# 64-bit weights made float32 by two VectorE instructions instead of three, and a gate made one ScalarE instruction

## The chip, the core and the metric

The kernel runs on one core of a Trainium2 chip. The core has five engines with a queue of instructions each, which runs in order: TensorE (PE, with its weight loads as PEld), VectorE (DVE), ScalarE (ACT), GpSimd (POOL) and SyncE (SP), which here only issues DMA transfers. They wait for one another by semaphores. The metric is the device time of one execution in microseconds (us); lower is better.

## What is computed

Attention with a block-causal mask over 4 batches, 8 heads, 576 positions and a head dimension of 64, then two feed-forward layers over the 2304 tokens. q, k, v are float32; the weights arrive as float64.

```python
scores = scale * np.matmul(q, k.transpose(0, 1, 3, 2))
scores = np.where(block_i >= block_j, scores, -1000000000.0)      # blocks of 64 positions
attn = softmax(scores)                                            # with 1e-9 added to the sum
x = heads_joined(attn @ v)                                        # 2304 x 512
h = x @ w_in;  g = np.maximum(h, 0.0) + alpha * np.minimum(h, 0.0);  x = g @ w_out      # layer 1: 512 x 2048, 2048 x 512
h = x @ w_in2; g = h * (1.0 / (1.0 + np.exp(-1.702 * h)));           out = g @ w_out2   # layer 2, same sizes
```

## The kernel before

**Number formats.** A float32 value is multiplied as a high and a low part (fp32r), three matmuls for each product. A weight tile of 128 x 512 arrives as 64-bit words (`load_w`, tile `rw`, 512 KB, two buffers). `narrow` (L163 to L179) makes it float32 in tile `sq`. A 64-bit float has 1 sign bit, 11 exponent bits and 52 fraction bits; its upper word (`wf[:, :, 1]`, every other 32-bit word of `rw`) holds all but the low 32 fraction bits. ScalarE scales the upper word, taken as a float32, by a power of two, which rebases the exponent (L171); VectorE shifts it left by 3 and masks (L174), puts the sign back (L176), and adds the top 3 bits of the lower word `wi[:, :, 0]` (L177). The integer scratch `wa` shares a tag of two buffers with other weight scratch. `split_w` or `comb` then make the high and low parts. There are 64 weight tiles, 32 of each layer.

**Stages.** (1) Attention, pass by pass (20 passes); beside it, as filler for TensorE, half of layer 1 in blocks of 288 tokens (`gemm1`, `gate`, `gate_split`, `g2_half`; eight of its sixteen slices of 128 hidden units), whose result goes to a DRAM scratch `xa`. A pass goes: scores on TensorE (L448), row extremes on VectorE (L462), exponentials on ScalarE (L472), and from pass 8 on high and low halves (L568, L573) in tile `hl`, which a transposing DMA (L577, issued by SP) turns into `pt`, and the product with v on TensorE (L599). (2) The other half of layer 1 in five units of up to 512 tokens, by a Strassen-like scheme with combined weights and inputs (tiles `ws`, `xc`; matmuls L843 into `ga` and `ep`; sums L891 to L894); `g2` (L918) accumulates into four `acc` banks of PSUM, and `block_out` adds what stage 1 left in `xa` (loaded to tile `o`, L927; added by VectorE, L928; stored to `x2s`, L929). The next unit's `g2` may write an `acc` bank only after that add; `o` has two buffers. (3) Layer 2 in five units of eight pairs of slices, in the same scheme.

**The gate.** `gate` (L232 to L242) makes g of h. Layer 1: ScalarE writes max(-h, 0) to `g`, VectorE combines it with h. Layer 2: ScalarE writes sigmoid(1.702 h) to `g` (L240), VectorE multiplies by h into the PSUM bank (L241). `gate_split` then has ScalarE write the high part of it (L140) and VectorE or GpSimd the low part (L143).

**What sets the order.** The code is recorded step by step with `at(kind, n, ...)`; each kind has a due place, shifted by a table of numbers `SHIFT`. `arrange` then runs a list scheduler with a cost for each instruction, and binds every engine's order to the result. So an engine's order is fixed when the program is built: an instruction whose input is late holds up all that stand behind it on its engine. Early in stage 1, 104 `warm` matmuls that compute nothing stand between the others.

Of the kernel before, what the change touches and what calls it, by code (L numbers as in the profile page):

```python
# [15 lines left out]
ACTF = mybir.ActivationFunctionType  # L16
ALU = mybir.AluOpType
# [40 lines left out]
    "split x 2": 8, "turn": 1.5, "turn out": 4.6, "pv t": 2, "sum t": 2.2, "sum out": 4.6, "out t": 4.5, "scale t": 5, "load w": 9, "load w 2": 9, "load x": 9, "load k": 9.5, "load q": 9.5, "load v": 9.5, "load alpha": 9.6,  # L58
}
SHIFT = {  # L60
    "comb 2": 232.8, "comb 3": -27.9, "first": 27.3, "gate": -98.0, "gate 0": -19.6, "gate 2": 67.8,
    "gemm1": 68.3, "gemm1 0": 171.6, "gemm2": 27.6, "half": 66.8, "half 0": 164.8, "half out": -68.7,
    "half out 0": 90.2, "high": 37.1, "load alpha": -25.6, "load k": 97.5, "load k 0": -174.1, "load q": 31.3,
    "load q 0": 127.5, "load v": -31.6, "load v 0": 140.7, "load w": -98.2, "load w 2": -24.0,
    "load w 3": 13.9, "load wc": -36.6, "load x": 132.4, "narrow": 100.5, "narrow 2": 19.6, "narrow 3": 96.5,
    "norm": 32.7, "norm 0": 111.8, "out": 26.7, "out t": -34.5, "prep out": 33.8, "prep out 0": 43.8,
    "prep t": 63.8, "prep t 0": -50.0, "prep v": 92.2, "pv": -64.1, "pv out": -63.9, "pv t": 43.2,
    "rest": -30.8, "scale t": 6.7, "score": -10.7, "score 0": -166.4, "second": 27.7, "setup": -15.8,
    "setup 2": -29.8, "snap": 1.4, "soft": -70.8, "soft 0": 17.8, "split g": -167.4, "split g 0": 68.9,
    "split g 2": 45.0, "split w": -71.7, "split w 2": 46.4, "split w 3": 58.0, "split x": 35.9,  # L70
    "split x 2": 84.1, "sum out": -41.5, "sum t": 28.5, "sums": -46.2, "turn": -70.2, "turn out": -30.2,
    "warm": 50.2,
}
BIG = 1.0e30

# [2 lines left out]
def kernel(  # L78
# [30 lines left out]
    scale = 1.0 / float(D) ** 0.5  # L109

    pe, dve, act, pool, sp = nc.tensor, nc.vector, nc.scalar, nc.gpsimd, nc.sync
# [51 lines left out]
    def narrow(u):  # L163

        src = words[u]
        wi = src.bitcast(I32).rearrange("p (n t) -> p n t", t=2)
        wf = src.bitcast(F32).rearrange("p (n t) -> p n t", t=2)
        sq = raw.tile([128, 512], F32, tag="sq", name="sq")  # L170
        act.activation(out=sq, in_=wf[:, :, 1], func=ACTF.Copy, scale=2.0 ** -112)  # L171
        hi = sq.bitcast(I32)
        a = raw.tile([128, 512], I32, tag="wc", bufs=2, name="wa")
        dve.tensor_scalar(out=a, in0=hi, scalar1=3, scalar2=0x7FFFFFF8, op0=ALU.logical_shift_left,  # L174
                          op1=ALU.bitwise_and)
        dve.scalar_tensor_tensor(out=a, in0=hi, scalar=-0x80000000, in1=a, op0=ALU.bitwise_and, op1=ALU.bitwise_or)  # L176
        dve.scalar_tensor_tensor(out=hi, in0=wi[:, :, 0], scalar=29, in1=a, op0=ALU.logical_shift_right,  # L177
                                 op1=ALU.bitwise_or)
        words[u] = sq  # L179

    def split_w(u, lo):
# [15 lines left out]
    pend = {}  # L197
# [11 lines left out]
    turn = []  # L209
# [22 lines left out]
    def gate(key, layer, f):  # L232
        ps, n = pend[key, f]
        g = gbuf(key, "g")[:, 0:n]
        to = ps if key[0] else g
        if layer == 0:
            act.activation(out=g, in_=ps, func=ACTF.Relu, scale=-1.0)
            dve.scalar_tensor_tensor(out=to, in0=g, scalar=nalph[:, f:f + 1], in1=ps, op0=ALU.mult, op1=ALU.add)  # L238
        else:
            act.activation(out=g, in_=ps, func=ACTF.Sigmoid, scale=1.702)  # L240
            dve.tensor_tensor(out=to, in0=g, in1=ps, op=ALU.mult)  # L241
        pend[key, f] = (to, n)  # L242

    def gate_split(key, f, lo, z=None):
        g, n = pend.pop((key, f))
# [178 lines left out]
    first = []  # L424
    place_ = []
    n = 0
# [183 lines left out]
    for u, (i, g, prods, part) in enumerate(slots):  # L610
        n = place_[u]
# [183 lines left out]
    wc = {}  # L795
# [456 lines left out]
```

## Time and profile before

| | |
|---|---|
| median of 3 runs | 1005.78 us (1004.87 to 1006.44) |
| profiled execution, its own time | 1003.02 us |
| span of its trace | 1001.2 us |
| mean granted TensorE clock | 0.998 of full speed |
| busy: PE | 978.1 us (98%) |
| busy: PEld, DVE | 859.7, 651.0 us |
| busy: ACT, POOL | 533.7, 351.9 us |
| HBM traffic over the span | 177 GB/s |

The profile is one execution. Busy time is the union of an engine's instructions; the time between them is idle, and the trace names what ended it. A view by stretches gives the busy time of every engine in each window; a view of waits gives who waited for whom; the timeline gives the instructions in order, with the idle time ahead of one in square brackets.

### The profile page before, as it was taken

Reading aid. Unit: us, or ns where it says so; the run is one execution under the profiler, and the core shown is the slowest. Engines: PE = TensorE matmul, PEld = TensorE weight load, DVE = VectorE, ACT = ScalarE, POOL = GpSimd, SP = SyncE. Lnnn points to the kernel's source line nnn. Section 1 sums busy time; section 2 is a strip of 40 time slices with the busy share of each in tenths; the row PEclk is TensorE's granted clock in tenths of the full one; section 3 lists DMA queues with packets and bytes.
Section 4 is the critical chain, followed back from the end, with each engine's and each line's share of the span. In section 5 each row is a group of like instructions: output and inputs, shape, how many; then the busy total and the mean of one; then the engine's idle time right before and its main releaser. Section 6 shows DMA issues by size and latency. Waiting matters only on the chain.

```text
span 1001.2 us, 21866 instructions
## 1 busy us (share of the span) xinstructions
PE 978.1 (98%) x8260; PEld 859.7 (86%) x8260; DVE 651.0 (65%) x1301; ACT 533.7 (53%) x1284; POOL 351.9 (35%) x396
## 2 busy tenths in 40 slices
PE   8999999999999999999999999999999999999998
PEld 5777787787788999999899889889999899899997
DVE  4788877786577566778778797887535534534332
ACT  4778777775777455565445555555423423433232
POOL 4346243442625156753426535233311311211000
PEclk9999999999999999999999999999999999999999
DMA  9635999999986866654656688987745756564360
GB/s 191 161 124 142 209 211 205 206 204 213 192 201 131 169 210 218 243 190 167 206 171 230 231 274 273 315 302 248 238 160 181 256 165 198 195 207 145 98 208 32
DMA packets 234648, 198.31 MB, mean 198 GB/s; under 512 B 146224, under 2 KB 172848, under 8 KB 234544
## 3 DMA queue, kind: packets, MB, share of 16 engines
q1 hardware_dynamic: 233216, 196.60, 69.2%
q8 instruction: 65, 1.06, 0.5%
q10 hardware_dynamic: 1328, 0.33, 0.2%
q14 instruction: 39, 0.32, 0.1%
HBM read 136.32 MB, written 40.89 MB: 177 GB/s over the span
## 4 chain that ended last, share of the span: by engine, by line
PE 81%; DMA 9%; ACT 3%; DVE 2%; POOL 2%; SPq 1%; issue 1%; POOLq 0%; ACTq 0%; DVEq 0%
PE acc L918 28%; PE ga L843 15%; PE ep L843 11%; PE h L223 7%; PE pv L599 3%; PE sc L448 3%; DMA pt<-hl 3%; PE x L268 3%; PE x L269 3%; PE x L270 3%; DMA wc<-wc 3%; PE pv L524 2%; PE tp L388 1%; DMA o<-xa 1%; PE s L448 1%
## 5 line engine op out<-in xcount | busy, mean ns | idle before, releaser
L918 PE MATMUL acc<-wh,gs 128*128 128x512 f32 x576 | 184.5, 391 | 2.1 <-DVE o L928 2.1
L843 PE MATMUL ga<-xc,ws 128*128 128x256 f32 x1368 | 184.2, 283 | 0.0
L843 PEld LDWEIGHTS ga<-xc,ws 128*128 128x128 f32 x1368 | 176.5, 191 | 4.6
L843 PE MATMUL ep<-xc,ws 128*128 128x256 f32 x936 | 130.7, 283 | 0.0
L918 PEld LDWEIGHTS acc<-wh,gs 128*128 128x128 f32 x576 | 108.3, 188 | 24.6 <-DVE o L928 2.9
L869 POOL TENSOR_TENSOR v<-u,v 128x256 f32<-128x256 f32 x48 | 40.5, 843 | 239.4 <-ACT v L868 239.3
L843 PEld LDWEIGHTS ep<-xc,ws 128*128 128x128 f32 x936 | 120.4, 192 | 0.4
L918 PE MATMUL acc<-wl,gs 128*128 128x512 f32 x288 | 112.6, 391 | 0.0
L867 ACT ACTIVATE u<-ga 128x512 f32<-128x512 f32 x48 | 28.6, 596 | 146.3 <-PE ga L843 146.3
L918 PE MATMUL acc<-gs,wh 128*128 128x512 f32 (+1 forms) x320 | 92.2, 371 | 2.1 <-DVE o L928 2.1
L891 DVE TENSOR_TENSOR u<-ep,v 128x256 f32<-128x256 f32 x48 | 20.2, 421 | 112.0 <-PE ep L843 111.7
L143 POOL TENSOR_TENSOR gs<-g,gs 128x288 fp32r<-128x288 f32 x64 | 56.1, 881 | 100.8 <-ACT gs L140 95.8
L223 PE MATMUL h<-xh,wh 128*128 128x288 f32 x256 | 78.8, 308 | 1.2 <-DVE g L238 1.1
L268 PE MATMUL x<-gs,wh 128*128 128x288 f32 x256 | 76.9, 304 | 0.5 <-ACT xo L274 0.3
L223 PE MATMUL h<-xlb,wh 128*128 128x288 f32 x256 | 77.1, 301 | 0.0
L269 PE MATMUL x<-gs,wh 128*128 128x288 f32 x256 | 76.2, 299 | 0.5 <-POOL gs L143 0.5
L223 PE MATMUL h<-xh,wl 128*128 128x288 f32 x256 | 76.4, 298 | 0.0
L270 PE MATMUL x<-gs,wl 128*128 128x288 f32 x256 | 76.1, 300 | 0.0
L462 DVE TENSOR_REDUCE stat<-sc 128x1 f32<-128x384 f32 (+7 forms) x128 | 55.1, 457 | 24.0 <-PE sc L448 22.2
L472 ACT ACTIVATE e<-sc,stat 128x384 f32<-128x384 f32 (+7 forms) x128 | 64.1, 511 | 7.4 <-DVE stat L462 6.6
L822 POOL TENSOR_TENSOR xt<-xr 128x512 f32<-128x512 f32 x40 | 55.2, 1389 | 35.6 <-DVE xc L143 13.5
L918 PEld LDWEIGHTS acc<-gs,wh 128*128 128x128 f32 x320 | 56.8, 189 | 11.2 <-DVE o L928 2.7
(118 smaller groups left out, 2146.6 us busy)
## 6 DMA issues: line engine op xcount, KB each, us to landing
ws<-wc SPq DMA_DIRECT2D x284, 256.0 KB, 3.9
wc<-wc SPq DMA_DIRECT2D x84, 256.0 KB, 3.3
rw<-in_moe_w_in_dram SPq DMA_DIRECT2D x32, 512.0 KB, 4.4
rw<-in_moe_w_out_dram SPq DMA_DIRECT2D x32, 512.0 KB, 4.1
xa<-xo SPq DMA_DIRECT2D x32, 144.0 KB, 3.3
out_dram<-o SPq DMA_DIRECT2D x18, 256.0 KB, 2.4
nat_k<-in_k_dram SPq DMA_DIRECT2D x32, 128.0 KB, 3.0
vt<-in_v_dram SPq DMA_DIRECT2D x32, 128.0 KB, 3.3
```

What stands on the lines that cost most here:

```text
L143: eng.tensor_tensor(out=dst, in0=src, in1=hi.bitcast(F32), op=ALU.subtract)
L223: pe.matmul(ps, st_[:, sl], mv[:, c], start=z == 0, stop=z == 3 * KD - 1)
L268: pe.matmul(ps, oh[:, sl], gh, start=f == 0, stop=False)
L269: pe.matmul(ps, oh[:, sl], gl, start=False, stop=False)
L270: pe.matmul(ps, ol[:, sl], gh, start=False, stop=f == NA - 1)
L448: pe.matmul(to[x:x + 64], qs[64 * h:64 * h + 64, 64 * y:64 * y + 64], ks[64 * h:64 * h + 64, k0:k0 + n], start=True, stop=True)
L462: dve.tensor_reduce(out=stat[:, 0, a:a + 1], in_=v, op=ALU.min, axis=AX.X if y < 8 else AX.XY)
L472: act.activation(out=eo if y < 8 else eo.rearrange("p (a b) -> p a b", a=2), in_=v, func=ACTF.Exp, scale=-1.0, bias=stat[:, 0, a:a + 1], a ...
L822: pool.tensor_tensor(out=x, in0=y, in1=y2, op=op)
L843: pe.matmul(ps, st_, mv, start=first and z == 0, stop=last and z == 5, skip_group_check=True)
L869: pool.tensor_tensor(out=v, in0=u[:, TH:TB], in1=v, op=ALU.subtract)
L918: pe.matmul(ps, a, b_, start=first and z == 0, stop=last and z == 2)
```

## The change

`narrow`: the ScalarE step becomes a leaky ramp (Prelu): a value of zero or more is scaled by 2^-112 as before, a negative one by 2^-112 times 2^32. The factor for negative values moves the exponent up by 32, so that after the shift left by 3 the sign bit comes out set; the instruction that put the sign back is gone. The remaining two on VectorE are a shift-and-mask of the lower word, which reads the 64-bit tile itself, and a shift-and-or. The tile `rw` is now read by the first VectorE instruction and not by the last.

`gate`, layer 2: ScalarE computes h times sigmoid(1.702 h) at once (Gelu_apprx_sigmoid) into `g`; the VectorE product is gone, `gate_split` reads `g` in SBUF and not the PSUM bank.

`SHIFT` has new values throughout, so `arrange` gives other orders on all engines. The instructions are otherwise the same in number and kind on PE, ACT, POOL and SP; DVE has 1157 instead of 1301.

```diff
-    "comb 2": 232.8, "comb 3": -27.9, "first": 27.3, "gate": -98.0, "gate 0": -19.6, "gate 2": 67.8,
...
+    "comb 2": -11.2, "comb 3": -22.2, "first": 27.1, "gate": -19.0, "gate 0": 39.3, "gate 2": -90.1,
...
-        act.activation(out=sq, in_=wf[:, :, 1], func=ACTF.Copy, scale=2.0 ** -112)
+
+        act.activation(out=sq, in_=wf[:, :, 1], func=ACTF.Prelu, scale=2.0 ** -112, alpha=2.0 ** 32)
         hi = sq.bitcast(I32)
         a = raw.tile([128, 512], I32, tag="wc", bufs=2, name="wa")
-        dve.tensor_scalar(out=a, in0=hi, scalar1=3, scalar2=0x7FFFFFF8, op0=ALU.logical_shift_left,
-                          op1=ALU.bitwise_and)
-        dve.scalar_tensor_tensor(out=a, in0=hi, scalar=-0x80000000, in1=a, op0=ALU.bitwise_and, op1=ALU.bitwise_or)
-        dve.scalar_tensor_tensor(out=hi, in0=wi[:, :, 0], scalar=29, in1=a, op0=ALU.logical_shift_right,
-                                 op1=ALU.bitwise_or)
+        dve.tensor_scalar(out=a, in0=wi[:, :, 0], scalar1=29, scalar2=7, op0=ALU.logical_shift_right, op1=ALU.bitwise_and)
+        dve.scalar_tensor_tensor(out=hi, in0=hi, scalar=3, in1=a, op0=ALU.logical_shift_left, op1=ALU.bitwise_or)
...
-        to = ps if key[0] else g
         if layer == 0:
             act.activation(out=g, in_=ps, func=ACTF.Relu, scale=-1.0)
+            to = ps if key[0] else g
             dve.scalar_tensor_tensor(out=to, in0=g, scalar=nalph[:, f:f + 1], in1=ps, op0=ALU.mult, op1=ALU.add)
-        else:
-            act.activation(out=g, in_=ps, func=ACTF.Sigmoid, scale=1.702)
-            dve.tensor_tensor(out=to, in0=g, in1=ps, op=ALU.mult)
-        pend[key, f] = (to, n)
+            g = to
+        else:
+            act.activation(out=g, in_=ps, func=ACTF.Gelu_apprx_sigmoid)
+        pend[key, f] = (g, n)
```

Three places show how the orders moved. Lines of the changed kernel are three lower than before from `gate` on, and buffers have other numbers.

TensorE, where the accumulators pass from the third full unit of layer 1 to the fourth (near 585 us of the trace). `acc_8815` to `acc_8817` are the first three banks, `acc_8767` to `acc_8769` the same banks in the changed kernel; `ga`, `ep` are matmuls of the scheme. Before:

```order
L918 MATMUL acc_8815<-gs_163,wh1_6123 128x512 x2
L918 MATMUL acc_8815<-gs_163,wl1_6124 128x512
L918 MATMUL acc_8816<-gs_163,wh1_6123 128x512 x2
L918 MATMUL acc_8816<-gs_163,wl1_6124 128x512
L843 MATMUL ga_8773<-xc_8512,ws_6936 128x256 x6
L843 MATMUL ga_8773<-xc_8515,ws_6932 128x256 x4
L918 MATMUL acc_8817<-gs_163,wh1_6093 128x512 x2
```

Changed:

```order
L915 MATMUL acc_8768<-gs_163,wh1_6097 128x512 x2
L915 MATMUL acc_8768<-gs_163,wl1_6098 128x512
L840 MATMUL ga_8725<-xc_8466,ws_6898 128x256 x6
L840 MATMUL ga_8725<-xc_8469,ws_6894 128x256 x6
L840 MATMUL ep_8726<-xc_8474,ws_6892 128x256 x6
L915 MATMUL acc_8767<-gs_163,wh1_6126 128x512
L915 MATMUL acc_8768<-gs_163,wh1_6126 128x512
L915 MATMUL acc_8769<-gs_163,wh1_6068 128x512 x2
```

The third bank is first written behind 10 matmuls of 256 columns before, behind 18 of them and two of 512 columns now.

VectorE, where the accumulators pass from layer 1 to layer 2 (near 630 us). `o_9292` and `o_9236` are the third of the unit's four adds; L174, L176, L177 (now L174, L175) are `narrow`; L891 to L894 (now L888 to L891) are sums of a pair. Before:

```order
L174 TENSOR_SCALAR wa_9033<-sq_9031 128x512
L143 TENSOR_TENSOR gs_163<-ep_9213,gs_163 128x512
L176 SCALAR_TENSOR_TENSOR wa_9033<-sq_9031,wa_9033 128x512
L174 TENSOR_SCALAR wa_9160<-sq_9158 128x512
L177 SCALAR_TENSOR_TENSOR sq_9031<-rw_8985,wa_9033 128x512
L176 SCALAR_TENSOR_TENSOR wa_9160<-sq_9158,wa_9160 128x512
L891 TENSOR_TENSOR u_9424<-ep_9355,v_9425 128x256
L143 TENSOR_TENSOR wl1_9043<-sq_9031,wh1_9042 128x512
L892 TENSOR_TENSOR u_9424<-u_9424,ga_9354 128x256
L893 TENSOR_TENSOR ep_9355<-ep_9355,u_9424 128x256
L894 TENSOR_TENSOR ga_9354<-ga_9354,u_9424 128x256
L928 TENSOR_TENSOR o_9292<-acc_8817,o_9292 128x512
```

Changed:

```order
L175 SCALAR_TENSOR_TENSOR sq_9147<-sq_9147,wa_9149 128x512
L889 TENSOR_TENSOR u_9222<-u_9222,ga_9156 128x256
L890 TENSOR_TENSOR ep_9157<-ep_9157,u_9222 128x256
L891 TENSOR_TENSOR ga_9156<-ga_9156,u_9222 128x256
L142 TENSOR_TENSOR wl1_9153<-sq_9147,wh1_9152 128x512
L142 TENSOR_TENSOR gs_163<-g_9277,gs_163 128x512
L142 TENSOR_TENSOR gs_163<-g_9279,gs_163 128x512
L925 TENSOR_TENSOR o_9236<-acc_8769,o_9236 128x512
L174 TENSOR_SCALAR wa_9246<-rw_9196 128x512
L175 SCALAR_TENSOR_TENSOR sq_9244<-sq_9244,wa_9246 128x512
L925 TENSOR_TENSOR o_9240<-acc_8770,o_9240 128x512
L888 TENSOR_TENSOR u_9364<-ep_9295,v_9365 128x256
```

The third add stood behind the sums of the next pair (`ep_9355`); it now stands ahead of them (`ep_9295`), and so does the fourth.

VectorE, first pass of attention (near 10 us): `sc_281` are its scores, `rw_605` is the first weight tile, `sq_655` what ScalarE makes of it. Before:

```order
L462 TENSOR_REDUCE stat0_189<-sc_281 128x1 x2
L406 COPY k0_266<-tp_292 128x384
L462 TENSOR_REDUCE stat0_189<-sc_281 128x1 x3
L500 COPY pe_375<-et_347 128x128
L174 TENSOR_SCALAR wa_657<-sq_655 128x512
```

Changed:

```order
L459 TENSOR_REDUCE stat0_189<-sc_281 128x1 x3
L403 COPY k0_266<-tp_292 128x384
L459 TENSOR_REDUCE stat0_189<-sc_281 128x1
L174 TENSOR_SCALAR wa_657<-rw_605 128x512
L459 TENSOR_REDUCE stat0_189<-sc_281 128x1
```

The first instruction on a weight tile now waits for the transfer of `rw` itself and not for ScalarE, and stands between reductions of the scores.

## Rows read from the trace of the kernel before

**Rows 1.** Windows: stretch, length, busy time (count) per engine, clock, DMA, GB/s.

```profile
0.00:25.00 25.00, 20.91 (x157) 13.31 (x157) 11.35 (x33) 11.17 (x34) 11.43 (x36) 0.94 0.94 191
25.00:125.00 100.00, 97.92 (x1051) 76.81 (x1050) 83.40 (x179) 75.31 (x190) 40.12 (x44) 1.00 0.62 159
125.00:275.00 150.00, 141.91 (x1932) 114.70 (x1934) 107.20 (x257) 108.35 (x315) 63.30 (x69) 1.00 1.00 206
...
575.00:650.00 75.00, 70.86 (x447) 63.54 (x446) 62.76 (x111) 38.70 (x74) 28.81 (x30) 1.00 0.85 285
650.00:950.00 300.00, 300.00 (x1879) 272.23 (x1879) 153.85 (x281) 115.51 (x221) 63.96 (x71) 1.00 0.62 201
950.00:1001.00 51.00, 47.20 (x286) 42.00 (x284) 15.17 (x39) 17.17 (x45) 0.00 (x0) 1.00 0.37 119
sum 1001.00, PE 978.07 PEld 859.73 DVE 650.99 ACT 533.71 POOL 351.91; mean PE 122.26 PEld 107.47 DVE 81.37 ACT 66.71 POOL 43.99
```

**Rows 2.** Waits of PE: who waited for whom, us in total, times, longest.

```profile
PE pv L599 <- DMA pt<-hl: 5.9, 6, 1.8
PE acc L918 <- DVE o L928: 4.1, 4, 1.7
```

**Rows 3.** Timeline of PE: start, length, what, count [idle before <- what ended it].

```profile
174.81 1.39 PE L599 MATMUL pv<-pt,vp 128*64 128x256 f16 x43 [1.72 <-DMA pt<-hl]
...
587.40 0.73 PE L918 MATMUL acc<-gs,wh 128*128 128x512 f32 x2 [1.60 <-DVE o L928]
...
589.13 0.88 PE L843 MATMUL ep<-xc,ws 128*128 128x256 f32 x6
589.85 1.60 PE L843 MATMUL ga<-xc,ws 128*128 128x256 f32 x12
...
592.15 0.73 PE L918 MATMUL acc<-gs,wh 128*128 128x512 f32 x2 [0.46 <-DVE o L928]
...
636.45 0.50 PE L918 MATMUL acc<-wh,gs 128*128 128x512 f32 x1 [1.71 <-DVE o L928]
```

**Rows 4.** Groups of DVE: instruction, count | busy us, mean ns | idle before.

```profile
L177 DVE SCALAR_TENSOR_TENSOR sq<-rw,wa 128x512 int32<-128x512 int32 x64 | 53.0, 828 | 1.2
L176 DVE SCALAR_TENSOR_TENSOR wa<-sq,wa 128x512 int32<-128x512 int32 x64 | 52.1, 814 | 1.2
...
L174 DVE TENSOR_SCALAR wa<-sq 128x512 int32<-128x512 int32 x64 | 30.9, 483 | 17.3 <-ACT sq L171 12.6 <-DMA wc<-wc 3.2 <-DMA o<-xa 0.7
L241 DVE TENSOR_TENSOR ga<-g,ga 128x512 f32<-128x512 f32 (+1 forms) x40 | 25.7, 642 | 30.2 <-ACT g L240 30.1
L241 DVE TENSOR_TENSOR ep<-g,ep 128x512 f32<-128x512 f32 (+1 forms) x40 | 25.5, 637 | 0.8 <-ACT g L240 0.6
```

**Rows 5.** Windows, instructions of L174 alone: stretch, length, DVE busy (count), clock, DMA.

```profile
25.00:125.00 100.00, 8.32 (x16) 1.00 0.62 159
125.00:275.00 150.00, 1.77 (x4) 1.00 1.00 206
...
575.00:650.00 75.00, 4.58 (x10) 1.00 0.85 285
```

**Rows 6.** Timeline of SP, DMA issues in the stretch 160 to 176 us.

```profile
166.54 2.24 SPq L158 DMA_DIRECT2D rw<-in_moe_w_in_dram  x1
168.88 3.81 SPq L577 DMA_TRANSPOSE pt<-hl  x1
```

**Rows 7.** Timeline of DVE in the stretch 630 to 642 us.

```profile
633.79 0.42 DVE L891 TENSOR_TENSOR u<-ep,v 128x256 f32<-128x256 f32 x1
...
635.72 0.68 DVE L928 TENSOR_TENSOR o<-acc,o 128x512 f32<-128x512 f32 x1
```

**Rows 8.** Waits of ACT for weight transfers: us in total, times, longest.

```profile
ACT sq L171 <- DMA rw<-in_moe_w_out_dram: 8.9, 8, 3.2
...
ACT sq L171 <- DMA rw<-in_moe_w_in_dram: 7.3, 5, 2.4
```

**Rows 9.** Group of ACT on the weight words.

```profile
L171 ACT ACTIVATE sq<-rw 128x512 f32<-128x512 f32 x64 | 42.2, 669 | 16.9 <-DMA rw<-in_moe_w_out_dram 8.9 <-DMA rw<-in_moe_w_in_dram 7.3 <-DVE wl L143 0.7
```

More of the change, by code (lines that the diff above doesn't have):

```diff
@@ L60 @@
 SHIFT = {
-    "comb 2": 232.8, "comb 3": -27.9, "first": 27.3, "gate": -98.0, "gate 0": -19.6, "gate 2": 67.8,
[L62 to L72, printed above, removed]
+    "comb 2": -11.2, "comb 3": -22.2, "first": 27.1, "gate": -19.0, "gate 0": 39.3, "gate 2": -90.1,
+    "gemm1": 75.3, "gemm1 0": 264.6, "gemm2": 27.4, "half": 73.5, "half 0": 154.4, "half out": -8.9,
+    "half out 0": -68.9, "high": 65.0, "load alpha": -19.0, "load k": 11.5, "load k 0": -144.8,
+    "load q": 41.1, "load q 0": -3.3, "load v": 46.5, "load v 0": 85.1, "load w": -131.1, "load w 2": -0.6,
+    "load w 3": 48.6, "load wc": -35.6, "load x": -10.8, "narrow": 23.3, "narrow 2": 28.9, "narrow 3": -94.2,
+    "norm": 80.0, "norm 0": 112.9, "out": 8.8, "out t": -0.1, "prep out": 42.0, "prep out 0": -35.2,
+    "prep t": 76.8, "prep t 0": 120.4, "prep v": 4.3, "pv": 64.5, "pv out": -57.6, "pv t": 17.6, "rest": -6.9,
+    "scale t": -52.2, "score": -106.3, "score 0": -69.4, "second": 27.1, "setup": -36.2, "setup 2": 7.2,
+    "snap": -30.4, "soft": 3.7, "soft 0": -48.3, "split g": -11.9, "split g 0": 4.8, "split g 2": -32.6,
+    "split w": 38.7, "split w 2": 16.6, "split w 3": 25.7, "split x": -2.9, "split x 2": 41.2,
+    "sum out": -15.1, "sum t": -31.8, "sums": -37.0, "turn": -96.8, "turn out": 2.1, "warm": 60.0,
 }
```

## The prediction

> **What bounds the kernel now.** I read the windows by stage first [rows 1], because a share over the whole span mixes stages with different limits. TensorE is busy 978.1 us of a span of 1001.2, so only 23.1 us are idle. They lie in five places: 25.00 - 20.91 = 4.1 us in the first 25 us, 2.1 from 25 to 125, 8.1 from 125 to 275, 4.1 from 575 to 650, and 3.8 behind the last matmuls (the rest has 0.9 in all). From 650 to 950 TensorE is busy for 300.00 of 300.00 us. VectorE, which the change relieves, is the busiest of the others where attention runs beside the weight work (83.40 of 100 us) and around 600 us (62.76 of 75), but it is no bound by itself in any stage. So the change is worth what it takes from TensorE's waits, and no more.
>
> The view of TensorE's waits [rows 2] then says which of them VectorE feeds. 5.9 us go to the transposing DMAs that bring the attention weights to L599, 4.1 us to the add L928 that frees an accumulator bank. The first ends on a DMA, the second on VectorE. The timeline shows single ones: 1.72 us ahead of L599, and 1.60, 0.46 and 1.71 us at two changes of unit [rows 3].
>
> **The first part, narrow.** Each weight tile costs VectorE 483 + 814 + 828 ns = 2.13 us in three instructions, and 64 of them 136 us [rows 4]. Afterwards it is one instruction on one tile and one on two. The second has the form of L176, 814 ns. The first has the form of L174 (483 ns) but reads every other word, as L177 does in one of its inputs (828 ns). These are the two ends: the relief is between 2.13 - 1.64 = 0.48 us and 2.13 - 1.30 = 0.83 us for a tile. I take 0.81, near the upper end, because L177 with its stride costs only 14 ns more than L176 without one; a stride of two words hardly shows there. That is 52 us of VectorE in all, of which 16 tiles or 13 us from 25 to 125, 4 tiles or 3 us from 125 to 275, and 10 tiles or 8 us from 575 to 650 [rows 5]. All of it lies beside TensorE's work.
>
> L177 reads every other word at the pace of L176 [rows 4]. [...]
>
> On ScalarE one instruction takes the place of one. The trace has no Prelu; the nearest row is the Copy on the same words, 669 ns [rows 9]. If it cost nothing more, nothing changes; if it cost twice as much, ScalarE would have 16 x 0.67 = 10.7 us more from 25 to 125, 86 of 100 us [rows 1], still below VectorE now. I take 669 ns. Both orders hold two table loads, so no switch of tables is added.
>
> The tile `rw` is now let go by the first VectorE instruction, at least 0.81 us earlier. What stands behind its next load is the SP queue: from 166.54 us a weight load held SP for 2.24 us, and the transposing DMA behind it was issued at 168.88 [rows 6]; TensorE waited 1.72 us at 174.81 [rows 3]. This is a real lever on the 5.9 us, but only 4 of the 64 tiles fall from 125 to 275 [rows 5].
>
> **The second part, the gate of layer 2.** It takes 80 products off VectorE, 25.7 + 25.5 = 51.2 us [rows 4]. Nearly all of them lie between 600 and 1001 us, where TensorE does not wait: cost and gain zero. The cover is the 300.00 us of TensorE's work; VectorE has 153.85 of them and ScalarE 115.51 [rows 1]. The low part now reads two SBUF tiles instead of one in PSUM; even if each of the 80 took as long again as the product that is gone, VectorE would be where it was. The PSUM banks come free earlier, and nobody waits for them there.
>
> **The third part, the orders.** TensorE's instructions are the same in number and kind, so its busy time stays; I leave it at 978.1. What moves are the waits.
>
> From 575 to 650: at the change of unit near 587 us the third bank is written behind 8 more matmuls of 256 columns and two of 512. Six of the former take 589.85 - 589.13 = 0.72 us [rows 3], 0.12 each; with two of double width that is 8 x 0.12 + 2 x 0.24 = 1.4 us more cover for a wait of 1.60, and the fourth bank's 0.46 us goes with it. I keep 0.2. At the change near 636 us the third add ran at 635.72, behind the sums of the next pair, whose first started only at 633.79 [rows 7]. In the new order it stands ahead of them, so it can run up to 1.9 us sooner; but TensorE asks for that bank 31 matmuls of 256 columns, 3.7 us, sooner as well (it stood behind 42 of them, now behind 11). The loads of `o`, too, stand nearer to the stores ahead of them on SP. Between all covered, 0, and 1.71 + 3.7 - 1.9 = 3.5 us I take 1.4 for this change. So the stretch keeps 1.6 of 4.1 us: -2.5, with ends of -4.1 and -0.4.
>
> From 125 to 275: the same chain from scores over VectorE and SP to L599 is planned again, with 3 us less on VectorE and a weight load that holds SP for less time. I take -1.0 of 8.1; the ends are -4 (half of the waits go) and +4 (half as much again, since the orders differ throughout).
>
> From 25 to 125: VectorE goes from 83 to 70 us of 100. Of 2.1 us I take 0.5 off, with ends of -2.1 and +2.
>
> The first 25 us and the last 3.8 us: the same loads, the same filler matmuls, the same last matmuls and stores. I take 0, with 1 us either way for the loads' order.
>
> The sum is -2.5 - 1.0 - 0.5 = -4.0 us. The profiled execution took 1003.02 us, 1.8 more than its span of 1001.2, and so would come to 999.0. The median of the runs is 2.8 above that execution, and the prediction is for the median: 1005.8 - 4.0 = **1001.8 us**.
>
> **The rivals.**
> No change: the new orders pay what the old ones paid. For it: most of the idle time in the attention stage ends on DMAs [rows 2], not on VectorE, and there are few tiles there. Then 125 to 275 keeps 8.1, 25 to 125 keeps 2.1, and from 575 to 650 the worse end holds, 0.2 + 3.5 = 3.7: -0.4, or 1005.4 us. Against it: the order at both changes of unit moved the way that the waits ask for.
>
> Slower: VectorE stands before weights that have not landed. Its first instruction on a tile now waits for the transfer itself, and in the first pass it stands between two reductions of the scores; what is queued behind it is the softmax, and TensorE behind that. ScalarE waited for such transfers 13 times, 16.2 us in all, 1.25 us each [rows 8]. The place is 25 to 125 us. VectorE would have 100 - 70.4 = 29.6 us to spare there, or 1.85 us for each of 16 tiles, and from that point on it delays TensorE one for one. At 1.25 us it costs nothing. At 2.4 us, the longest wait for an input weight, it costs 16 x 2.4 - 29.6 = 8.8 us, and with the other -3.5 the time is 1011.1. Against it: 1.25 is well under 1.85, and an earlier freed `rw` lets loads start sooner.
>
> Larger gain: half of the waits from 125 to 275 go (-4), all from 575 to 650 (-4.1), half from 25 to 125 (-1): 996.7 us. For it: both are fed by VectorE or by SP behind it.
>
> That the strided instruction is slow (828 ns, relief 0.48 us) is a rival of the mechanism but not of the time: VectorE still has 16 x 0.48 = 8 us less to do from 25 to 125, and the forecast moves by some tenths.
>
> **How the numbers follow.** Forecast 0.48, own range 1000 to 1004; no change 0.24; slower 0.16; larger gain 0.12. The prediction is the forecast's, 1001.8. A measurement of this kernel can tell about 0.2%, 2.0 us. Faster by more: 0.48 + 0.12, less the edge of the forecast that falls inside, 0.58. Within: 0.24. Slower by more: 0.16 and the upper edge of no change, 0.18. For 8 in 10 I go from 996, which leaves out less than half of the larger gain, to 1009.5, which leaves out most of the slower case.
>
> **What would show it.** In the profile of the changed kernel: the first instruction of `narrow` near 0.5 us and the second near 0.8; VectorE near 550 us busy; TensorE still near 978; PE's wait for L925 (the add) at 1 to 2 us instead of 4.1, and for the transposing DMA near 5; 300 of 300 us from 650 to 950. The forecast is wrong if TensorE's waits for the transposing DMAs or for VectorE's reductions grow by more than 4 us, if VectorE idles behind `rw`, or if the stage from 650 on shows idle time on TensorE.

## The result, and the profile of the changed kernel

The changed kernel takes 1017.88 us (median of 4 runs, 1015.71 to 1020.61) against 1005.33 us (4 runs): a ratio of 1.0128, 95% interval 1.0096 to 1.0161. It is slower by 12.5 us, where the prediction had 4 us faster and a range that ended at 1009.5. The profiled execution took 1015.71 us with a span of 1013.9.

Windows of the changed kernel, as [rows 1]: stretch, length, busy time (count) of PE, PEld, DVE, ACT, POOL, then clock, DMA, GB/s.

```profile
0.00:25.00 25.00, 19.28 (x155) 12.51 (x156) 10.53 (x30) 10.47 (x31) 11.46 (x35) 1.00 0.94 187
25.00:125.00 100.00, 96.06 (x1034) 74.75 (x1034) 69.45 (x168) 76.06 (x195) 41.30 (x44) 0.98 0.67 171
125.00:275.00 150.00, 138.24 (x1818) 113.70 (x1816) 105.79 (x245) 105.72 (x312) 66.53 (x69) 0.98 0.92 210
275.00:350.00 75.00, 75.00 (x927) 63.06 (x928) 44.48 (x111) 48.10 (x139) 22.75 (x25) 1.00 0.64 126
350.00:575.00 225.00, 221.94 (x1664) 209.14 (x1661) 149.23 (x266) 117.97 (x266) 114.86 (x121) 1.00 0.61 200
575.00:650.00 75.00, 69.45 (x431) 61.87 (x430) 54.35 (x96) 37.31 (x71) 34.19 (x32) 1.00 0.86 295
650.00:950.00 300.00, 300.00 (x1885) 272.51 (x1884) 118.37 (x215) 117.05 (x225) 71.29 (x72) 1.00 0.62 203
950.00:1014.00 64.00, 60.26 (x364) 53.71 (x363) 13.07 (x30) 19.68 (x50) 0.74 (x1) 1.00 0.37 115
sum 1014.00, PE 980.22 PEld 861.24 DVE 565.27 ACT 532.37 POOL 363.13; mean PE 122.53 PEld 107.65 DVE 70.66 ACT 66.55 POOL 45.39
```

Length less PE's busy time, stretch by stretch, against [rows 1], gives where the 12.7 us of span come from:

| stretch | idle before | idle after | difference | predicted |
|---|---|---|---|---|
| 0 to 25 | 4.1 | 5.7 | +1.6 | 0 |
| 25 to 125 | 2.1 | 3.9 | +1.9 | -0.5 |
| 125 to 275 | 8.1 | 11.8 | +3.7 | -1.0 |
| 275 to 575 | 0.7 | 3.1 | +2.3 | 0 |
| 575 to 650 | 4.1 | 5.6 | +1.4 | -2.5 |
| 650 to the end | 4.0 | 3.6 | -0.4 | 0 |
| PE's busy time | 978.1 | 980.2 | +2.1 | 0 |

VectorE has 86 us less to do, and TensorE waits more in nearly every stage. Its waits, as [rows 2]:

```profile
PE pv L596 <- DMA pt<-hl: 9.7, 8, 3.1
PE acc L915 <- DVE o L925: 4.4, 3, 2.6
PE x L265 <- DVE g L235: 3.6, 3, 2.1
PE et L487 <- ACT e L469: 2.7, 3, 1.8
```

The longest is 3.1 us for a transposing DMA at 205 us. Timelines of the changed kernel there; first PE (start, length, what, count [idle before <- what ended it]):

```profile
200.27 1.19 PE L445 MATMUL sc<-ks,qt 64*64 64x288 f32 x8 [1.09 <-ACT e L469]
...
204.99 1.28 PE L596 MATMUL pv<-pt,vp 128*64 128x128 f16 x20 [3.08 <-DMA pt<-hl]
```

then the last VectorE work on that DMA's input, and SP's issues:

```profile
183.83 1.63 DVE L570 SCALAR_TENSOR_TENSOR hl<-e,stat,hl 128x448 f16<-128x448 f32 x2
```

```profile
181.95 4.37 SPq L574 DMA_TRANSPOSE pt<-hl  x1
...
188.86 1.05 SPq L356 DMA_DIRECT2D nat_q<-in_q_dram  x2
189.96 4.69 SPq L574 DMA_TRANSPOSE pt<-hl  x1
...
197.07 0.55 SPq L157 DMA_DIRECT2D rw<-in_moe_w_in_dram  x1
197.67 3.48 SPq L574 DMA_TRANSPOSE pt<-hl  x1
```

The input was complete at 183.83 + 1.63 = 185.46 us. SP came to the transposing DMA at 197.67, 12.2 us later: two other transposing DMAs of 4.37 and 4.69 us, and loads and stores, stood ahead. This wait of TensorE comes from the SP queue's order; a faster VectorE would not have shortened it. Matched in the same way by the order of the program, three more of the waits (121.68, 162.78 and 196.04 us) have an input that was ready 6.2 to 7.8 us before SP came to it. Not all are SP's: at 147.31 us, a wait of 0.7 us, SP came 0.6 us after the input.

The granted clock of the same place, in windows:

```profile
195.00:202.45 7.45, 4.84 (x74) 3.64 (x72) 4.67 (x12) 5.39 (x21) 2.83 (x4) 1.00 0.85 195
202.45:209.28 6.83, 4.29 (x49) 4.22 (x50) 2.57 (x6) 0.83 (x2) 1.51 (x2) 0.50 0.86 223
```

After a wait of 1.09 us and in the middle of that of 3.08 us the clock fell to 0.50 until 209.28. The matmuls of L220 with 288 columns start 0.24 us apart there (207.41 to 208.85 us) and 0.13 us apart behind it (210.14 to 211.86 us). By that, an estimate, about half of the 4.29 us busy there is added time, which is most of the +2.1 us of PE's busy time. (One stretch of 3.4 us at half clock between 21 and 29 us, in which TensorE is busy throughout, stands in both traces and cancels.) The wait is paid twice.

The instructions of `narrow` and of the low part, group by group (count | busy us, mean ns | idle before), as [rows 4] and [rows 9]:

```profile
L142 DVE TENSOR_TENSOR gs<-g,gs 128x512 fp32r<-128x512 f32 (+1 forms) x80 | 55.1, 699 | 90.4 <-ACT gs L139 90.4
...
L175 DVE SCALAR_TENSOR_TENSOR sq<-sq,wa 128x512 int32<-128x512 int32 x64 | 52.7, 825 | 6.0 <-ACT sq L171 4.9
...
L174 DVE TENSOR_SCALAR wa<-rw 128x512 int32<-128x512 int32 x64 | 36.7, 573 | 32.3 <-DMA rw<-in_moe_w_out_dram 19.0 <-DMA rw<-in_moe_w_in_dram 6.3 <-DMA wc<-wc 4.9
```

```profile
L171 ACT ACTIVATE sq<-rw 128x512 f32<-128x512 f32 x64 | 42.4, 676 | 29.6 <-DMA rw<-in_moe_w_out_dram 18.0 <-DMA rw<-in_moe_w_in_dram 10.8 <-POOL wc L742 0.5
```

### The profile page after: what moved, and what is told of

It is laid out like the page before. It is cut to its first block, busy times and chain, and to the rows that moved or that the text cites. A ratio compares the mean times of both kernels' runs of the same rounds, so it can differ in the third digit from the quotient of the medians.

```text
span 1013.9 us, 21666 instructions
## 1 busy us (share of the span) xinstructions
PE 980.2 (97%) x8260; PEld 861.2 (85%) x8260; DVE 565.3 (56%) x1157; ACT 532.4 (53%) x1284; POOL 363.1 (36%) x396
## 4 chain that ended last, share of the span: by engine, by line
PE 70%; DMA 12%; DVE 6%; ACT 5%; issue 2%; POOL 2%; SPq 2%; DVEq 0%; ACTq 0%; POOLq 0%
PE acc L915 25%; PE ga L840 13%; PE ep L840 9%; PE h L220 6%; DMA wc<-wc 5%; PE pv L596 3%; PE sc L445 3%; PE x L265 3%; PE x L266 2%; PE x L267 2%; DMA pt<-hl 2%; DMA rw<-in_moe_w_out_dram 2%; DMA rw<-in_moe_w_in_dram 2%; SPq L356 1%; ACT e L469 1%
## 5 line engine op out<-in xcount | busy, mean ns | idle before, releaser
L142 DVE TENSOR_TENSOR gs<-g,gs 128x512 fp32r<-128x512 f32 (+1 forms) x80 | 55.1, 699 | 90.4 <-ACT gs L139 90.4
L139 ACT ACTIVATE gs<-g 128x288 fp32r<-128x288 f32 (+2 forms) x144 | 74.3, 525 | 15.9 <-DVE g L235 14.6
L220 PE MATMUL h<-xh,wh 128*128 128x288 f32 x256 | 79.6, 311 | 0.2 <-DVE g L235 0.2
L888 DVE TENSOR_TENSOR u<-ep,v 128x256 f32<-128x256 f32 x48 | 20.2, 420 | 105.6 <-PE ep L840 105.6
L220 PE MATMUL h<-xlb,wh 128*128 128x288 f32 x256 | 77.8, 304 | 0.0
L220 PE MATMUL h<-xh,wl 128*128 128x288 f32 x256 | 76.9, 301 | 0.0
L596 PEld LDWEIGHTS <-vp 128*64 128x64 bf16 x1680 | 46.7, 112 | 24.1 <-issue 13.2
```

The costliest lines, as they stand in the source:

```text
L139: act.activation(out=dst, in_=src, func=ACTF.Copy, scale=scale_)
L142: eng.tensor_tensor(out=dst, in0=src, in1=hi.bitcast(F32), op=ALU.subtract)
L220: pe.matmul(ps, st_[:, sl], mv[:, c], start=z == 0, stop=z == 3 * KD - 1)
L596: pe.matmul(o, l, r, start=z < 2, stop=z >= len(ops) - 2)
```

## The experiments

The change has three parts: the two edits, and a table that gives every engine another order. Theory A: the order costs, the edits don't. Theory B: the edits cost, because VectorE now stands before weights that have not landed (25.3 us of idle time ahead of L174 above). To tell them apart, a kernel can have its orders written down in place of planned ones; `placed` returns an engine's instructions in a recorded order:

```diff
+    orders = {e: placed(e, todo) for e in names}
     for order in orders.values():
         for a, b in zip(order, order[1:]):
```

All runs have both edits unless another code is named, and each is compared with the kernel before on the same chip.

| run | code | order | us, median | ratio to before (95%) |
|---|---|---|---|---|
| f1 | both edits | before | 1007.70 | 1.0018 (0.9995 to 1.0040) |
| f2 | narrow alone | before | 1005.92 | 1.0018 (0.9996 to 1.0039) |
| f3 | gate alone | changed | 1062.60 | 1.0565 (1.0534 to 1.0596) |
| f4 | both edits | planned with the old table | 1020.53 | 1.0165 (1.0132 to 1.0198) |
| h1 | both edits | changed to 300 us, then before | 1019.99 | 1.0151 (1.0126 to 1.0176) |
| h2 | both edits | before to 300 us, then changed | 1014.35 | 1.0101 (1.0074 to 1.0128) |
| h3 | both edits | changed to 120 us, then before | 1011.88 | 1.0062 (1.0043 to 1.0082) |
| a1 | both edits | changed, six moves | 1011.14 | 1.0070 (1.0057 to 1.0084) |
| o1 | both edits | before, adds sooner | 1004.06 | 0.9994 (0.9977 to 1.0010) |
| p1 | both edits | o1, six transposes sooner | 1007.07 | 1.0027 (1.0005 to 1.0048) |
| p2 | both edits | p1, a bank later | 1005.76 | 1.0015 (0.9997 to 1.0033) |
| p3 | before | p2 | 1007.51 | 1.0042 (1.0026 to 1.0059) |
| p4 | both edits | o1, four transposes sooner | 1006.03 | 1.0022 (1.0004 to 1.0040) |
| p5 | before | p4 | 1007.70 | 1.0028 (1.0009 to 1.0047) |
| p6 | both edits | o1, three transposes sooner | 1004.52 | 0.9989 (0.9972 to 1.0006) |
| p7 | before | p6 | 1003.54 | 0.9985 (0.9968 to 1.0003) |

**The edits in the old order (f1, f2).** The recorded order is that of before, with the 144 removed instructions left out; f2 has only the edit in `narrow`.

> Both edits (narrow with two VectorE instructions, the gate of layer 2 as one ScalarE instruction), but every engine's order written down as it stands in the kernel before, with the 144 removed VectorE instructions left out. Theory A (the new order costs, the edits don't): 1000 to 1006 us; VectorE near 565 us busy, TensorE's idle time between 20 and 25 us as before, VectorE's idle time behind rw in places, but none of it reaching TensorE. Theory B (the edits cost, because VectorE now stands before weights that have not landed): 1011 to 1018 us, with TensorE's idle time up by 6 us or more behind VectorE.

> narrow alone with two VectorE instructions, the old gate, every engine's order as in the kernel before. Theory A: 1000 to 1006 us, and within 1 us of the kernel with both edits in the old order, because layer 2's stage keeps TensorE busy for 300 of 300 us either way. Theory B: 1011 to 1018. If the gate's edit costs (its g stays longer in a tile of two buffers), this one is faster than both edits together by more than 2 us.

Measured: 1.0018 both times. The medians, 1007.70 and 1005.92, differ by 1.8 us where 1 was expected, and f1's lies 1.7 us above Theory A's range and 3.3 below Theory B's. In f1's profile TensorE is idle 23.2 us (span 1003.2 less 980.0 busy; 23.1 before), and VectorE is busy 570.9 us. Its waits for the transposes and for the adds, then VectorE's group on the weights:

```profile
PE pv L596 <- DMA pt<-hl: 8.1, 7, 2.2
PE acc L915 <- DVE o L925: 5.1, 3, 3.1
```

```profile
L174 DVE TENSOR_SCALAR wa<-rw 128x512 int32<-128x512 int32 x64 | 33.9, 532 | 12.9 <-DMA rw<-in_moe_w_out_dram 10.9 <-DMA wc<-wc 1.3 <-DMA rw<-in_moe_w_in_dram 0.7
```

Theory B falls for this order: VectorE stands before the transfers for 11.6 us here, and TensorE's idle time is what it was. The first half of Theory A, that the edits don't cost, holds, with what hurts the prediction: 80 us less of VectorE's work gain nothing. Its other half, that the new order costs without the edits too, was for f3 to show. The two waits of [rows 2] are still there, a little longer.

**The new order with the old narrow (f3), and a new plan with the old table (f4).** f3 takes the part of the diff in `narrow` back and keeps the recorded order of the changed kernel, with all three old instructions where its second one stood. f4 takes the part on `SHIFT` back and lets `arrange` plan:

```diff
-    "comb 2": -11.2, "comb 3": -22.2, "first": 27.1, "gate": -19.0, "gate 0": 39.3, "gate 2": -90.1,
+    "comb 2": 232.8, "comb 3": -27.9, "first": 27.3, "gate": -98.0, "gate 0": -19.6, "gate 2": 67.8,
...
```

> The changed kernel's order on every engine, with the new gate, but the old narrow: its three VectorE instructions stand one behind the other where the changed kernel has its second one (so VectorE waits for ScalarE there and never for rw itself). Theory A: still 1013 to 1022 us, as the changed kernel. Theory B: the loss goes with the direct wait for rw, 1004 to 1009 us.

> Both edits with the table SHIFT of before; the order is planned again with the two edits' costs, so it differs from both orders throughout. Theory A: the time is a draw among orders planned with one table, 1002 to 1014 us, and it differs from the kernel with the same edits in the old order; its excess over that one lies in TensorE's waits from 25 to 275 us and near the changes of unit. Theory B: 1011 to 1018 us, like every order with these edits.

f3 missed by 40 us. SP's waits (the queue's own, us in total, times, longest) show what differs from the changed kernel:

```profile
SPq L157 <- DVE sq L176: 70.5, 20, 6.6
SPq L159 <- DVE sq L176: 60.6, 15, 7.0
```

A weight load waits at SP's head until the last of the three lets `rw` go, and everything behind it waits too: 131 us, where the changed kernel has 47.7 us for its L174. That this is the cause is argued, not shown: the kernel before has 102.6 us of the same wait (59.5 and 43.1, for its L177) and takes 1005.3 us. This run adds a late release to that order, so it can't be used for the split, and whether the new order costs as much with the old code stays open. f4 came out 6.5 us over its range. So with both edits the planned orders stand at 1.0128 (new table) and 1.0165 (old table), and the order of before at 1.0018.

**Which part of the new order (h1, h2, h3).** Every engine first runs what one plan (of the two kernels) had started by a given time, in the other plan's order, and behind that the rest in the first plan's order, written down row by row as in f1.

> Both edits. Every engine runs in the changed kernel's order what the old plan had started by its 300th us (attention and the layer-1 work beside it), and in the order of before all that is behind. Theory A1 (the new order costs where attention runs): the idle time of TensorE was 21.4 us in the first 275 us with the new order and 12.3 with the old one, 0 against 1.6 from 275 to 350, so about 7.5 of the 10 us come with this half: 1013 to 1017 us. Theory A2 (it costs at the changes of unit and behind 350 us): 1005 to 1009 us.

> Both edits; the same cut the other way: the order of before for what the new plan had started by its 300th us, the changed kernel's order behind. Theory A1: TensorE's idle time behind 350 us was 3.4 us longer with the new order, so 1009 to 1012 us. Theory A2: 1014 to 1019 us. If the two halves together give much more or much less than 10 us over the kernel with both edits in the old order, the seam itself costs and the split can't be read.

> Both edits; the changed kernel's order only for what the old plan had started by its 120th us (loads, first passes, the weights of layer 1), the order of before behind. Theory A1: idle time of TensorE in the first 125 us was 9.6 us with the new order and 5.1 with the old, so 4 to 5 us over the kernel with both edits in the old order, 1010 to 1013 us. If the loss lies in the transposed attention passes from 125 to 275 instead: 1005 to 1009 us.

h1 and h2 lie 12 and 7 us over f1, together 19 instead of 10: the seam between the two orders costs, as the expectation allowed for, and the split at 300 us can't be read. h2's trace has a wait of 2.3 us at 331 us (for `ks`) that neither plan has. h3 came as expected, 4.2 us over f1. Its longest waits beside those for `pt` and `o` are the changed kernel's own:

```profile
PE et L487 <- ACT e L469: 2.7, 3, 1.8
PE x L265 <- DVE g L235: 2.1, 1, 2.1
```

In the first 120 us TensorE is idle for 8.8 us in h3's profile, 8.7 in the changed kernel's and 3.9 in f1's. So some 4 of the 10 us go with the order of the first 120 us, if h3's seam costs little: scores and exponentials of the first pass one behind the other, and one gate at 100 us whose ScalarE instruction stands behind three splits of the next input.

**SP's order in the changed kernel (a1).** Five transposing DMAs move ahead of loads, and that gate ahead of the splits. One of the moves on SP, and ScalarE's:

```diff
 L272 DMA xa<-xo 128x288
+L574 DMA_TRANSPOSE pt<-hl_186 128x18x128
+L574 DMA_TRANSPOSE pt<-hl_187 128x14x128
 L356 DMA nat_q_175<-in_q_dram 128x4x64
...
+L233 ACTIVATE g<-h 128x288
 L139 ACTIVATE xh<-x 128x288 x3
-L233 ACTIVATE g<-h 128x288
```

> The changed kernel with five transposing DMAs moved ahead of loads on SP (passes near 115, 148, 155, 190 and 198 us, their hl ready 2 to 12 us before SP came to them in the changed kernel) and one gate's ScalarE instruction ahead of the three input splits that stood before it near 99 us. Theory SP: about 7 of its waits' 9.3 us at these six places go and the stretch of half clock near 203 us with them: 1008 to 1012 us. If its loss lies elsewhere in the order, or the waits only move: 1014 to 1019 us.

1011.14 us, within the expectation: 6 us of the 12.5 come back without a change of any instruction. The waits:

```profile
PE x L265 <- DVE g L235: 2.9, 4, 1.3
PE h L220 <- DVE g L235: 2.8, 2, 1.8
PE pv L596 <- DMA pt<-hl: 1.5, 4, 0.6
```

That for `pt` falls from 9.7 to 1.5 us, and the granted clock is 1.00 in every window up to 575 us (0.98 from 25 to 275 us in the changed kernel's); 2.8 us come in new (`h`). The windows from 125 to 275 us, f1 and then a1:

```profile
125.00:275.00 150.00, 142.82 (x1902) 115.39 (x1901) 103.41 (x250) 106.68 (x312) 63.07 (x68) 0.98 0.99 202
125.00:275.00 150.00, 142.78 (x1897) 117.23 (x1896) 111.28 (x258) 107.72 (x318) 67.87 (x71) 1.00 0.97 217
```

TensorE is idle there for 7.2 us in both, against 11.8 in the changed kernel: SP's order explains the loss of this stretch. In the first 125 us a1 keeps 9.4 of 9.7 us, so the gate's move gained nothing.

**The add at the changes of unit (o1).** In the old order, on SP (and, at the second of the two changes, the third and fourth add on VectorE ahead of all but the first of the next pair's sums):

```diff
-L926 DMA x2s<-o 128x512
+L926 DMA x2s<-o 128x512 x2
...
+L924 DMA o<-xa 128x512 x2
 L783 DMA ws<-wc_5_1_142 128x512
 L783 DMA ws<-wc_5_5_146 128x512
-L926 DMA x2s<-o 128x512
-L924 DMA o<-xa 128x512
```

> Both edits in the order of before, with one thing moved at the last two changes of unit of layer 1: on SP the second store of o stands right behind the first and the loads of the third and fourth o stand together and sooner; on VectorE the third and fourth add stand ahead of the next pair's sums. If the wait of TensorE for the add (5.1 us in the kernel with both edits in the old order) is one of order: it falls to 2 to 3 us and the time to 1004 to 1006 us. If it is one of the transfer (the queues are 0.9 busy there and a load of o takes 4.5 us): it stays at 4 to 5 us, and so does the time.

The time fell as expected, to 0.9994 (f1: 1.0018, and the intervals overlap), but the wait is 4.5 us, not 2 to 3, so the gain isn't shown to come from it. At the first of the two changes VectorE stood 2.24 us before the load of `o`, issued by SP at 584.21 us, until the add could start at 588.70; there the wait is for the transfer.

**SP's order in the kernel before (p1 to p7).** o1's trace has the same pattern as the changed kernel: for a product at 181.81 us, which waited 1.89 us, the input was complete at 165.90 + 1.21 = 167.11, and SP came to it at 173.90:

```profile
165.90 1.21 DVE L570 SCALAR_TENSOR_TENSOR hl<-e,stat,hl 128x448 f16<-128x448 f32 x2 [0.46 <-ACT hl L565]
```

```profile
173.90 3.29 SPq L574 DMA_TRANSPOSE pt<-hl  x1
```

p1 moves that one and five others up, p2 also moves six matmuls on TensorE, and p3 is p2's order with the code of before. On SP for that product, and on TensorE:

```diff
 L574 DMA_TRANSPOSE pt<-hl_188 128x18x128
-L272 DMA xa<-xo 128x288 x2
+L574 DMA_TRANSPOSE pt<-hl_186 128x18x128
+L272 DMA xa<-xo 128x288 x2
+L574 DMA_TRANSPOSE pt<-hl_187 128x14x128
...
-L840 MATMUL ga<-xc,ws 128x256 x10
+L840 MATMUL ga<-xc,ws 128x256 x12
+L840 MATMUL ep<-xc,ws 128x256 x6
+L840 MATMUL ga<-xc,ws 128x256 x12
 L915 MATMUL acc<-gs,wh_6068 128x512 x2
```

> Both edits, the order of the run o1_add_sooner, and on SP six transposing DMAs moved ahead of loads and stores that stood before them (attention passes near 112, 117, 168, 174, 236 and 243 us); nothing else. In o1 their input hl had been ready 3 to 7 us before SP came to them. Theory SP (TensorE's waits for pt are SP's order, not VectorE's work): those waits fall from 7.3 us to 2 to 3, the stretch of half clock behind the wait at 181.8 us goes, and the time is 997 to 1001 us, below both kernels. Rival (the transfer itself or the buffers of pt bound it, or the loads set back are late in their turn): 1002 to 1007 us.

> As p1_transposes_sooner, and on TensorE the first six matmuls into the third accumulator bank at the last-but-one change of unit of layer 1 stand behind 20 matmuls of 256 columns that stood after them. In o1 TensorE waited 2.6 us there for the add, whose load of o lands late. If that cover takes the place of the wait: 1 to 2.5 us below p1. If the banks of the next pair are not free by then: the same as p1 or slower.

> The code of before (narrow with three VectorE instructions, the gate of layer 2 with VectorE's product) in exactly the order of p2_bank_later. Theory A (the edits are worth nothing, order is all): within 2 us of p2. If the relief of VectorE counts once SP is out of the way: 3 to 6 us slower than p2.

p1 missed and came out at the upper end of the rival's range. Its profile, the slowest of its 11 executions (1012.50 us), has waits for `pt` of 3.9 us (p2: 1.1), and two others take their place:

```profile
PE h L220 <- DVE g L235: 3.9, 2, 2.8
...
PE sc L445 <- ACT qt L139: 2.8, 1, 2.8
```

p2's median is 1.3 us below p1's, as expected, but the add's wait there stays (2.0 us; p1: 2.2) and 1.1 us for `gs` come in: banks that were not free took the cover. p3 is 0.27% slower than p2 by the ratios, whose intervals overlap, and 1.75 us by the medians, inside Theory A's 2 us. p4 kept the loads of q and the stores of `xo` in their place, and p5 is its order with the old code:

```diff
 L574 DMA_TRANSPOSE pt<-hl_186 128x18x128
-L157 DMA rw<-in_moe_w_in_dram 128x4x128
 L272 DMA xa<-xo 128x288
 L574 DMA_TRANSPOSE pt<-hl_187 128x14x128
-L157 DMA rw<-in_moe_w_in_dram 128x4x128
+L157 DMA rw<-in_moe_w_in_dram 128x4x128 x2
```

> Both edits, the order of the run o1_add_sooner, and on SP four transposing DMAs sooner (near 117, 168, 174 and 236 us), this time only ahead of weight loads, the store of x and scratch stores: the stores of xo and the loads of q that gave way in p1_transposes_sooner, and whose users then waited (2.8 us for qt, 2.8 us for a gate behind xo), keep their place. Theory SP: waits for pt of 3 us or less, no new wait over 1.5 us from 100 to 260 us, 999 to 1002 us, below both kernels. Rival (each transfer moved up sets back one that is as urgent): 1004 to 1007 us.

> The code of before in exactly the order of p4_few_sooner. If VectorE's relief is worth nothing: within 1.5 us of p4. If it is worth what p2_bank_later and p3_old_edits differ by, and more once SP is out of the way: 2 to 4 us slower than p4.

p4 missed as well, within the rival's range, and its trace shows what the move above costs. VectorE, then PE:

```profile
123.09 0.43 DVE L174 TENSOR_SCALAR wa<-rw 128x512 int32<-128x512 int32 x1 [3.80 <-DMA rw<-in_moe_w_in_dram]
...
124.47 0.51 DVE L235 SCALAR_TENSOR_TENSOR g<-g,nalph,h 128x288 f32<-128x288 f32 x1 [0.36 <-ACT g L233]
```

```profile
125.04 0.40 PE L220 MATMUL h<-xh,wh 128*128 128x288 f32 x1 [3.40 <-DVE g L235]
```

This is the slower rival of the prediction, with its place: an engine stands before a weight that has not landed, a gate stands behind it, and TensorE behind the gate. But the old code has it too. ScalarE in p5:

```profile
122.44 0.66 ACT L171 ACTIVATE sq<-rw 128x512 f32<-128x512 f32 x1 [4.03 <-DMA rw<-in_moe_w_in_dram]
```

TensorE waited 3.8 us there. ScalarE stood before the transfer already, and the gate's first half stands behind it. What sets the price here is where the load stands on SP, not which engine reads it first. p6 takes the one move back; p7 is its order with the old code.

> As p4_few_sooner, without its first move: the transposing DMA near 117 us goes back behind the weight load that it had passed. In p4 that load then landed 3.3 us later, VectorE and ScalarE both stood 3.8 and 4.4 us before it, a gate stood behind them, and TensorE waited 3.4 us at 125 us with a stretch of half clock behind. Theory SP: that wait becomes one of about 1 us for pt at 122 us, the stretch of half clock goes, and the time is 3 to 5 us below p4: 1001 to 1003 us. Rival (the time of these orders is scatter that no single move explains): 1004 to 1007 us.

> The code of before in exactly the order of p6_weights_kept. If VectorE's relief is worth nothing: within 1.5 us of p6. If it is worth the 1 to 2 us by which the last two pairs differed: 1 to 2 us slower than p6, for the third time.

The wait of 3.4 us is gone, and the ratio falls from 1.0022 to 0.9989; the median, 1004.52, lies 1.5 us below p4's, above the 1001 to 1003 expected and in the range of the rival, scatter that no single move explains. The waits for `pt` are 7.2 us again (p4: 5.1). p7 is at 0.9985. Neither beats the kernel before by more than can be told. So no move of transposes on SP is shown to gain anything in the order of before; a1, in the new order, is the one run in which it did. Four orders now have both codes: the edits cost 0.18% in the order of before (f1), gain 0.27% (p2 against p3) and 0.06% (p4, p5), and cost 0.04% (p6, p7). On average that is nothing, a gain of 0.03%. From the scatter of the runs I estimate that each difference is known to about 0.2%, and their mean to 0.1%.

## Why the prediction was wrong

**The step that failed** is the third part, the orders. The sum put -2.5 us on the changes of unit, where I had compared the orders row by row, -1.0 and -0.5 on the stretches from 125 to 275 and from 25 to 125 us, where I had not, and nothing on all the rest. Measured are +1.4, +3.7 and +1.9, and +1.6 and +2.3 us of waits where I had nothing (the first 25 us, and from 275 to 575). Two terms came out near their worse ends of +4 and +2, and the changes of unit beyond theirs, -0.4. With both edits in the old order the time is 1.0018 of the kernel before (f1), so the 10 us from there to the changed kernel come with the new order. The changed kernel's profile has 4.6 us more idle time of TensorE than f1's in the first 125 us (h3 has them too), 4.6 more from 125 to 275, where SP comes to the transposes too late (a1 takes these back), and 1.3 more from 275 to 575. The last was read from the windows and from no run of its own.

**"Fed by VectorE or by SP behind it"** was the second error: I let VectorE's 13 us of relief from 25 to 125 us and 3 us from 125 to 275 shorten TensorE's waits. In f1 VectorE has the relief, and TensorE's idle time from 25 to 125 us is 2.9 instead of 2.1, from 125 to 275 it is 7.2 instead of 8.1: 10.1 against 10.2 together. The rows were there: SP's timeline [rows 6] showed a load ahead of a transposing DMA, and the time at which that DMA's input was ready had to be set beside it. I priced the load's 2.24 us as a lever of `rw`'s earlier release and did not ask what stands ahead of the other transposes in the new order.

**The changes of unit.** Near 587 us (now 599) I was right that the add's wait goes, and didn't name what is late next. PE there, and at the change to layer 2:

```profile
599.37 1.35 PE L915 MATMUL acc<-gs,wh 128*128 128x512 f32 x4 [1.18 <-ACT gs L139]
...
603.82 1.34 PE L840 MATMUL ep<-xc,ws 128*128 128x256 f32 x9 [0.52 <-DVE gs L142]
...
644.48 0.50 PE L915 MATMUL acc<-wh,gs 128*128 128x512 f32 x1 [2.56 <-DVE o L925]
...
648.85 0.50 PE L915 MATMUL acc<-wh,gs 128*128 128x512 f32 x1 [1.29 <-DVE o L925]
```

1.18 + 0.52 us for `gs` take the place of 2.06 us [rows 3]. At the change to layer 2 I kept 1.4 us, with 3.5 as the worse end; it is 2.56 + 1.29 = 3.85. The third add stood behind two low parts, which had waited 1.24 us for ScalarE, and the fourth waited for its own load, which SP issued at 641.27 for an add at 648.11.

**Right, and worth nothing.** `narrow` now takes 573 + 825 = 1398 ns a tile and not 2.13 us [rows 4]: a relief of 0.73 us, where I had 0.81. The strided first instruction has a median of 427 ns, against 424 for the old one without a stride: a step of two words hardly shows here, as [rows 4] had suggested. The mean did rise, from 483 to 573 ns, but beside GpSimd: the 34 of the 64 instructions that overlap none of GpSimd's take 420 ns on average (419 before, 43 of them), the 30 that do take 747 (615 before, 21). ScalarE's Prelu costs 676 ns for 669 [rows 9]. VectorE came to 565.3 us and not 550: the smaller relief is 5 us of that, and the low part of layer 2, which takes 699 ns from SBUF where 634 and 630 were the means from PSUM, another 5 (80 x 67 ns); the remaining 5 are not accounted for. The low parts show the same neighbour: of the 64 with 512 columns that read SBUF alone, 33 beside no GpSimd instruction take 691 ns and 31 beside one 849, while those that read PSUM take 679 to 683 either way. The stage from 650 to 950 us kept TensorE busy for 300.00 of 300.00, as predicted. Of the signs that would show the forecast wrong, VectorE did idle behind `rw` (25.3 us), and the waits for the transposing DMAs grew by 3.8 us, just short of the 4 that I had set.

**TensorE's busy time** was taken as fixed. It rose by 2.1 us, by the estimate above mostly in the stretch at a clock of 0.50 from 202.45 to 209.28 us.

**The slower rival** (1011.1) had the right sign and a real mechanism (p4). Its cause, VectorE as the first reader, costs nothing in the old order (f1), and in p4's order the old code pays as much (p5). In the changed order no run separates it, since f3 can't be used. VectorE stood there longest, 5.77 us, before the weight at 379.37 us (ScalarE before the same one for 3.68), and TensorE waited 1.27 us for a gate at 388.69; whether one follows from the other is not shown.

## What to carry to other kernels

A wait of the bottleneck engine that ends on a DMA can be owed to the queue that issued it (a1, where the waits for `pt` fell from 9.7 to 1.5 us), to the transfer itself (o1, 2.24 us before a load of `o`) or to a late input (0.7 us at 147.31 us of the changed kernel's trace): put the time at which the transfer's input was ready beside the time at which the queue came to it, before any relief elsewhere is counted as a gain. In p1 and p4 transfers that moved up set others back, and TensorE waited for those instead (2.8 us for `qt` in p1, 3.4 us for a gate behind a weight in p4). An order that a planner makes anew is a change of its own and is to be priced as one, with a spread that covers the whole program and not only the places one has compared. To test an edit, run it in the old order, written down row by row.

## What the hardware showed that I had not expected

A wait of TensorE was often paid twice here. In the changed kernel's trace the granted clock fell to 0.50 in two stretches within TensorE's work, from 24.96 to 28.37 us, behind a wait of 1.89 us, and from 202.45 to 209.28 us; behind its waits of 1.81, 1.92, 2.11 and 2.56 us it stayed at 1.00. In the 18 profiles (before, after and the 16 runs) it fell to 0.50 in 52 stretches within TensorE's work; at 51 of them TensorE had just ended a wait of 1.65 to 3.85 us, or was still in it. Of 84 waits of more than 1.7 us, 49 were followed by such a stretch and 35 were not. This may be part of why the same kernel scatters: of the 112 runs of the kernel before that go with the experiments, 40 with a mean clock of 0.998 average 1003.9 us and 20 with 0.995 average 1006.0. It is not all of it: single runs lie between 1000.3 and 1012.2 us, and one with 0.946 took 1005.8. The changed kernel's four runs have 0.992 to 0.995.

A transposing DMA holds SP for long: 1.5 to 4.7 us each in the changed kernel's trace, 107 us for 36 of them, in a queue that also carries every weight load.
